# A fused linear attention and gated expert layer: one table of task order and engines replaced by another

## The chip, the cores and the metric

The kernel runs on one core of a Trainium2 chip. The metric is the device time of one execution in microseconds; of several runs the median is given. The core has five engines with queues of their own: TensorE (PE, matmuls), VectorE (DVE), ScalarE (ACT), GpSimd (POOL) and SyncE (SP, which here only issues DMA transfers).

## The reference

Four batches of four heads, 1088 tokens each, head size 32. Keys and queries become 64 features (an outer product of two projections of 8), the keys' features are summed against the values, and a query's features are multiplied by that sum and divided by a denominator. The 4352 tokens x 128 channels that come out are normalized and go through a gated layer with 1536 inner columns.

```python
a = np.einsum('rd,bhsd->bhsr', S1, x)
b = np.einsum('rd,bhsd->bhsr', S2, x)
phi = np.einsum('bhsi,bhsj->bhsij', a, b).reshape(*x.shape[:-1], r * r)
kv = np.einsum('bhsf,bhsd->bhfd', k_p, v)
z = np.sum(k_p, axis=2)
num = np.einsum('bhsf,bhfd->bhsd', q_p, kv)
den = np.einsum('bhsf,bhf->bhs', q_p, z)[..., None] + 1e-06
...
rms = np.sqrt(np.mean(x * x, axis=-1, keepdims=True) + 1e-06)
xn = x / rms * rms_g
g = xn @ w_gate
silu = g * (1.0 / (1.0 + np.exp(-g)))
val = xn @ w_val
return (silu * val @ w_out)
```

## The kernel before

All of the program is one core's. Tokens are worked through in nine chunks (eight of 512 columns, one of 256), the inner columns in twelve groups of 128.

*Attention.* For a batch, the key side loads keys (`kt`) and values (`vt`), projects the keys (L519 for batch 0, L497 for the others), forms features `phi` (L452, L539) and sums them against the values (L531, the "key products"), whose sums are copied to `kv` (L556, L560). For a chunk, the query side projects the queries (L594 for chunks 0 and 1, L622 for the others), forms `phiq` (L452 and transposes L602; or from chunk 2 by a round trip over `far` in HBM, read back as `at` and `bt`, and the product L651), multiplies by `kv` (L678, the "numerators"), adds to the denominator (`den`, L698 or L699), divides, takes the mean square (L709), its root on POOL (L721), scales (`xn`, L724 or L731), and transposes (L758, or over `turned` in HBM) to `x`, which is split into a rounded part `x_hi` and a rest `x_lo`.

*Experts.* A slot is one chunk with one group of inner columns: three matmuls (hi x hi, lo x hi, hi x lo) for the gate `g_ps` and three for the value `v_ps` (L802), silu on ACT (L811, `s`), the product `h` on DVE (L814), a cast to `h_hi` (L350 on ACT or L351 on DVE), a subtraction to `h_lo` (L832 on DVE or POOL) and three output matmuls (L840). The last two groups of the last chunk use a plain f32 `h` (L821). `g_ps` and `v_ps` have two buffers each, so TensorE may run two accumulators of each kind ahead. The weights of a group come as 64-bit words (`w_raw`, L422) and are converted in five steps (`w_top`, `w_full`, `w_hi`, `w_lo`).

*What sets the order.* The program is a list of 1259 tasks. `ORDER` is a permutation of their numbers: instructions are emitted in that order, and each engine runs its own in the order in which they were emitted. `ON` holds one letter (a, d, p for ACT, DVE, POOL) for each task that has more than one possible engine. `Plan.follow` walks through ORDER with a planned occupancy and latency for each task (`Way`); from these planned times come the buffer slot that a tile gets, the waits between DVE and POOL that keep their SBUF instructions apart, and the fillers: where it sees TensorE without work it emits short matmuls on zeros (`keep_warm`, L382). The chip does not read the planned times. Each engine waits for the semaphores of what an instruction needs, and everything queued behind it waits as well.

Of the kernel before, what the change touches and what calls it, by code (L numbers as in the profile page):

```python
# [23 lines left out]
F = R * R  # L24
NT = B * S
P = 128
# [62 lines left out]
"""  # L89
ON = (  # L90
    "dapapadaddaadaadddaaaaapapdapapaadaadaadaapaadaadaadaadaddaadppddaapaadaaddadadadadadadadpdddaadddaaapapadadapapaadapa"
    "pddapapadapadapdpddddpadaaddadaapadaddpddadddadapadapddddadpadaadapaddpadapadddapapddadaaadpdaadpadadapddadddddapdpddd"
    "ddddddaaaapapapddapapdpdpddadaddpadadddaaaddddpapddadaddpadddapaddaddddaaddddpddapadadapadaddddpadpadddadadadadddapdda"
# [204 lines left out]
def attention_then_glu(ctx, tc, kT, v, qT, sw, w, out):  # L298
# [27 lines left out]
    def on_pool(n, emit, against=0):  # L326
        occ = n * 2.17 + 140
        return Way(occ, occ + 45, emit, True, against)
# [58 lines left out]
    def to_f32(n, dst, raw, top, reads, tt, writes):  # L387
# [18 lines left out]
        plan.add({"act": on_act(n, top_act, True), "dve": on_dve(n, top_dve, fast=True, against=100)}, reads, tt)  # L406
# [36 lines left out]
    def product(out, ab, m, writes, away=False):  # L443
# [7 lines left out]
        def outer(eng, a):  # L451
# [8 lines left out]
            "pool": on_pool(m * H * F * 0.85, lambda: outer(nc.gpsimd, both()[:, :m * H]), PHI_POOL),  # L460
        }, [both] if away else [ab, both], writes)

    def kside(b):
# [26 lines left out]
        if b in TURNED:  # L490
# [12 lines left out]
            for p in range(2):  # L503
                def turn(p=p):
                    nc.vector.transpose(out=kab()[:, :, p * NB // 2:(p + 1) * NB // 2], in_=pair[p]()[:, :g])

                dve(g, turn, [pair[p]], [(kab, p)])
        for i, (lo, hi) in enumerate(groups):
# [27 lines left out]
            if b in TURNED:  # L536
                def outer(eng, lo=lo, hi=hi, m=m):
# [9 lines left out]
                    "pool": on_pool(m * H * F * 0.85, lambda outer=outer: outer(nc.gpsimd), PHI_POOL),  # L547
# [24 lines left out]
    def qside(c):  # L572
# [94 lines left out]
        for u in range(0, nt, 2):  # L667
# [36 lines left out]
            for t in range(2):  # L704
                sq = sb("sq", [P, DM], 2)

                def mean(t=t, u=u, sq=sq):
                    one = x()[:, u + t]
                    nc.vector.tensor_tensor_reduce(  # L709
                        out=sq().rearrange("p (h d) -> p h d", h=H), in0=one, in1=one, scale=1.0 / DM, scalar=EPS, op0=ALU.mult, op1=ALU.add,  # L710
                        accum_out=ms()[:, u + t:u + t + 1],
                    )

                plan.add({"dve": Way(265, 345, mean, True)}, [(x, u)], [sq, (ms, u + t)])

        for u, wd in ((0, 2), (2, 2)) if first else ((0, nt),):
# [16 lines left out]
            plan.add({"pool": Way(400 + 150 * wd, 430 + 150 * wd, root)}, [(ms, i) for i in range(u, u + wd)], [(rstd, u)])  # L733
# [37 lines left out]
            plan.add({"act": Way(wd * 107 + 155, wd * 107 + 255, high)}, [*got, "gain"], [(x_hi, u)])  # L771
# [177 lines left out]
```

## Time and profile before

| | us |
|---|---|
| median of 3 runs | 252.35 |
| lowest, highest | 251.72, 253.43 |
| profiled execution | 254.73 |
| its span, first to last instruction | 252.6 |
| TensorE busy in it | 247.5 |
| DVE busy in it | 180.8 |
| ACT busy in it | 132.8 |
| POOL busy in it | 82.1 |

The span lacks the 2.1 us around it that the execution's time includes. An engine's busy time is the union of its instructions. PE is the matmul, PEld its weight load, which overlaps. The granted clock is the share of TensorE's full speed in a stretch.

### The profile page before, as it was taken

What the parts mean: (1) busy time and instruction counts of PE and PEld (TensorE: products, weight loads), DVE (VectorE), ACT (ScalarE), POOL (GpSimd) and SP (SyncE); (2) the same over time, 40 slices, a digit from 0 to 9 for tenths busy, and PEclk for the clock granted to TensorE, in tenths of its full rate; (3) what the DMA queues carried; (4) which work ended last, traced back from release to release, by engine and by line L of the source; (5) the groups of instructions that cost most, each with busy time, mean ns of one, the idle gap of its engine ahead of it and who ended that gap; (6) DMA issues with size and microseconds to landing.
All of it is one profiled execution on the core that took longest, in us unless ns stands there. A gap on an engine that the chain in (4) does not pass through costs nothing.

```text
span 252.6 us, 5870 instructions
## 1 busy us (share of the span) xinstructions
PE 247.5 (98%) x2244; PEld 199.9 (79%) x2244; DVE 180.8 (72%) x410; ACT 132.8 (53%) x287; POOL 82.1 (32%) x80
## 2 busy tenths in 40 slices
PE   7999999999999999999999999999999999999995
PEld 4878788786888788888888788887888888888895
DVE  1589998798566987775677688755679476774772
ACT  3477899744644537641546552644346555345351
POOL 4444332226543423105252401464341212142211
PEclk9799999999999999999999999999999999999999
DMA  6879994371354143330530235142002101020010
GB/s 226 288 245 294 335 273 141 95 212 33 78 170 113 33 123 104 92 96 21 142 89 1 47 93 169 31 127 94 3 0 44 42 3 42 0 84 3 0 42 21
DMA packets 19260, 25.55 MB, mean 101 GB/s; under 512 B 3105, under 2 KB 10657, under 8 KB 19233
## 3 DMA queue, kind: packets, MB, share of 16 engines
q1 hardware_dynamic: 18800, 24.54, 33.5%
q10 hardware_dynamic: 432, 0.66, 0.7%
q8 instruction: 17, 0.28, 0.5%
q14 instruction: 11, 0.08, 0.1%
HBM read 20.40 MB, written 4.78 MB: 100 GB/s over the span
## 4 chain that ended last, share of the span: by engine, by line
PE 96%; DMA 2%; SPq 0%; issue 0%; DVE 0%
PE v_ps L802 29%; PE g_ps L802 28%; PE o_ps L840 28%; PE att L678 3%; DMA q<-qT 2%; PE att L531 2%; PE att L622 1%; PE o_ps L531 1%; PE att L758 1%; PE att L594 1%; PE att L497 1%; PE g_ps L678 0%; PE att L602 0%; PE g_ps L602 0%; PE v_ps L678 0%; PE att L821 0%
## 5 line engine op out<-in xcount | busy, mean ns | idle before, releaser
L814 DVE TENSOR_TENSOR h<-v_ps,s 128x512 f32<-128x512 f32 (+2 forms) x110 | 69.8, 647 | 39.8 <-PE v_ps L802 27.5
L811 ACT ACTIVATE s<-g_ps 128x512 f32<-128x512 f32 (+1 forms) x108 | 61.0, 574 | 70.4 <-PE g_ps L802 37.7
L832 POOL TENSOR_TENSOR h_lo<-h,h_hi 128x512 fp32r<-128x512 f32 (+1 forms) x42 | 53.0, 1270 | 104.4 <-DVE h_lo L832 43.8
L350 ACT CAST h_hi<-h 128x512 fp32r<-128x512 f32 (+1 forms) x70 | 41.4, 602 | 19.9 <-DVE h L814 17.5
L832 DVE TENSOR_TENSOR h_lo<-h,h_hi 128x512 fp32r<-128x512 f32 (+1 forms) x64 | 41.4, 652 | 5.5 <-ACT h_hi L350 3.6
L802 PE MATMUL v_ps<-x_hi,w_hi 128*128 128x512 f32 (+1 forms) x110 | 41.9, 381 | 0.0
L802 PE MATMUL g_ps<-x_hi,w_hi 128*128 128x512 f32 (+1 forms) x110 | 41.8, 381 | 0.0
L802 PE MATMUL v_ps<-x_hi,w_lo 128*128 128x512 f32 (+1 forms) x110 | 41.6, 379 | 0.0
L802 PE MATMUL g_ps<-x_hi,w_lo 128*128 128x512 f32 (+1 forms) x110 | 41.6, 378 | 0.0
L802 PE MATMUL g_ps<-x_lo,w_hi 128*128 128x512 f32 (+1 forms) x110 | 41.5, 378 | 0.0
L802 PE MATMUL v_ps<-x_lo,w_hi 128*128 128x512 f32 (+1 forms) x110 | 41.3, 378 | 0.0
L840 PE MATMUL o_ps<-h_hi,w_hi 128*128 128x512 f32 (+1 forms) x106 | 40.9, 386 | 0.0
L840 PE MATMUL o_ps<-h_hi,w_lo 128*128 128x512 f32 (+1 forms) x106 | 40.8, 385 | 0.0
L840 PE MATMUL o_ps<-h_lo,w_hi 128*128 128x512 f32 (+1 forms) x106 | 40.8, 385 | 0.0
L802 PEld LDWEIGHTS v_ps<-x_hi,w_hi 128*128 128x128 f32 x110 | 20.7, 188 | 5.0 <-DVE w_lo L436 0.5
L802 PEld LDWEIGHTS g_ps<-x_hi,w_hi 128*128 128x128 f32 x110 | 20.7, 188 | 4.6
L802 PEld LDWEIGHTS v_ps<-x_hi,w_lo 128*128 128x128 f32 x110 | 20.7, 188 | 4.3
L802 PEld LDWEIGHTS g_ps<-x_hi,w_lo 128*128 128x128 f32 x110 | 20.7, 188 | 4.2
L802 PEld LDWEIGHTS g_ps<-x_lo,w_hi 128*128 128x128 f32 x110 | 20.6, 188 | 4.2
L802 PEld LDWEIGHTS v_ps<-x_lo,w_hi 128*128 128x128 f32 x110 | 20.5, 188 | 4.1
L840 PEld LDWEIGHTS o_ps<-h_lo,w_hi 128*128 128x128 f32 x106 | 19.9, 188 | 4.4
L840 PEld LDWEIGHTS o_ps<-h_hi,w_hi 128*128 128x128 f32 x106 | 19.9, 188 | 4.2
(112 smaller groups left out, 249.5 us busy)
## 6 DMA issues: line engine op xcount, KB each, us to landing
w_raw<-w SPq DMA_DIRECT2D x12, 384.0 KB
bt<-far SPq DMA_DIRECT2D x24, 128.0 KB
at<-far SPq DMA_DIRECT2D x12, 256.0 KB
q<-qT SPq DMA_DIRECT2D x7, 256.0 KB
turned<-xq SPq DMA_DIRECT2D x24, 64.0 KB
xt<-turned SPq DMA_DIRECT2D x6, 256.0 KB
outT<-o_sb SPq DMA_DIRECT2D x10, 128.0 KB
vt<-v SPq DMA_DIRECT2D x4, 272.0 KB
```

The costliest lines, as they stand in the source:

```text
L350: "act": on_act(n, lambda: nc.scalar.copy(out=out(), in_=in_()), True),
L497: nc.tensor.matmul(out=pair[p]()[a * D:(a + 1) * D, :g], lhsT=sblk[p * HALF:(p + 1) * HALF, p * NB // 2:(p + 1) * NB // 2], rhs=kt()[p * H ...
L531: nc.tensor.matmul(out=kvv[r0:r0 + wide, h // 2, :], lhsT=phi()[:, t, h * F + f:h * F + f + wide], rhs=vt()[:, t, h, :], start=(t == 0 and ...
L594: nc.tensor.matmul(out=ab()[hf * HALF:(hf + 1) * HALF, t * HALF:(t + 1) * HALF], lhsT=q()[:, s1:s1 + HALF], rhs=sblk, start=True, stop=True,)
L622: nc.tensor.matmul(out=accs[p]()[a * D:(a + 1) * D, :m], lhsT=sab[rows, p].rearrange("p c o r -> p (c o r)"), rhs=q()[rows, a * m:(a + 1) ...
L678: nc.tensor.matmul(out=nv[n0:n0 + wide, t, p, :], lhsT=phi()[:, p, l0:l0 + wide], rhs=kvs[(s0 + l0) // S][:, p, :], start=True, stop=True,)
L758: nc.tensor.transpose(out=xt()[:, t * P:(t + 1) * P], in_=xn()[:, t * DM:(t + 1) * DM], identity=ident)
L802: nc.tensor.matmul(out=acc()[:, cs], lhsT=wt[:, j, i3, :], rhs=x()[:, cs], start=(i == 0), stop=(i == 2))
L811: act(n, lambda: nc.scalar.activation(out=s()[:, :n], in_=gps()[:, :n], func=AF.Silu), cols(gps, whole[0]), [s])
L814: cs.stop - cs.start, lambda cs=cs: nc.vector.tensor_tensor(out=h()[:, cs], in0=vps()[:, cs], in1=s()[:, cs], op=ALU.mult),
L832: eng.tensor_tensor(out=h_lo()[:, :n], in0=h()[:, :n], in1=h_hi().bitcast(F32)[:, :n], op=ALU.subtract)
L840: nc.tensor.matmul(out=o_ps()[:, :n], lhsT=wt[:, j, 2, :], rhs=x()[:, :n], start=first and i == 0, stop=last and i == 2,)
```

## The change

Planned durations are altered in eight places (the conversion of weights on ACT, two products on POOL, the transposes on DVE, the mean square, the root on POOL, and the two parts of `x`), and the tables ORDER and ON are replaced. The code that the tasks emit is the same.

```diff
 ORDER = """
-1 0 2 6 9 3 14 10 15 4 32 33 7 37 16 5 64 34 18 38 19 12 26 27 22 20 146 39 28 147 11 23 24 151 35 40 41 65 17 13 148 21 25 36 29 152 153 149 66 72 67 30 73
...
+0 1 2 6 3 14 9 15 18 4 19 16 10 32 33 34 37 38 20 7 26 39 64 11 22 27 23 28 151 146 72 8 35 36 40 17 12 21 24 25 73 152 74 13 29 147 148 65 66 41 243 75 30 31
...
 ON = (
-    "dapapadaddaadaadddaaaaapapdapapaadaadaadaapaadaadaadaadaddaadppddaapaadaaddadadadadadadadpdddaadddaaapapadadapapaadapa"
...
+    "dapdpdddpadadaadadaaadapadaapddaadaadaadaapaadaapdadaadadpaaddppddadaddaaddadadadadadadaddpadaaddadaadddapapadddaaddda"
...
-        plan.add({"act": on_act(n, top_act, True), "dve": on_dve(n, top_dve, fast=True, against=100)}, reads, tt)
+        plan.add({"act": on_act(1.36 * n, top_act, True), "dve": on_dve(n, top_dve, fast=True, against=100)}, reads, tt)
...
-            "pool": on_pool(m * H * F * 0.85, lambda: outer(nc.gpsimd, both()[:, :m * H]), PHI_POOL),
+            "pool": on_pool(m * H * F * 0.8, lambda: outer(nc.gpsimd, both()[:, :m * H]), PHI_POOL),
...
-                dve(g, turn, [pair[p]], [(kab, p)])
+                dve(g + 14, turn, [pair[p]], [(kab, p)])
...
-                plan.add({"dve": Way(265, 345, mean, True)}, [(x, u)], [sq, (ms, u + t)])
+                plan.add({"dve": Way(215, 297, mean, True)}, [(x, u)], [sq, (ms, u + t)])
...
-            plan.add({"pool": Way(400 + 150 * wd, 430 + 150 * wd, root)}, [(ms, i) for i in range(u, u + wd)], [(rstd, u)])
+            plan.add({"pool": Way(150 + 270 * wd, 180 + 270 * wd, root)}, [(ms, i) for i in range(u, u + wd)], [(rstd, u)])
...
-            plan.add({"act": Way(wd * 107 + 155, wd * 107 + 255, high)}, [*got, "gain"], [(x_hi, u)])
-            dve(wd * P * 1.12, lambda low=low: low(nc.vector), [*got, "gain", (x_hi, u)], [(x_lo, u)], spread)
+            plan.add({"act": Way(wd * 118 + 140, wd * 118 + 240, high)}, [*got, "gain"], [(x_hi, u)])
+            dve(wd * P * 1.2, lambda low=low: low(nc.vector), [*got, "gain", (x_hi, u)], [(x_lo, u)], spread)
```

The three places below show what the tables move. Names carry a running number of the tile.

TensorE at the start, from the first filler on (g_ps and v_ps of L519: projections of batch 0's keys; att of L594: projections of the query chunks 0 and 1, `q_109` in two halves). Before:

```order
L382 MATMUL o_ps_97<-const-float32-0.0 1x96
L519 MATMUL g_ps_124<-sblk,kt_106 64x64 x2
L382 MATMUL o_ps_97<-const-float32-0.0 1x32
L594 MATMUL att_130<-sblk,q_109 64x64 x4
L382 MATMUL o_ps_97<-const-float32-0.0 1x128
L594 MATMUL att_144<-sblk,q_109 64x64 x4
L519 MATMUL v_ps_151<-sblk,kt_106 64x64 x6
L519 MATMUL v_ps_162<-sblk,kt_106 64x64 x4
L519 MATMUL g_ps_170<-sblk,kt_106 64x64 x6
```

And now:

```order
L382 MATMUL o_ps_97<-const-float32-0.0 1x96
L519 MATMUL g_ps_124<-sblk,kt_106 64x64 x2
L519 MATMUL v_ps_129<-sblk,kt_106 64x64 x6
L594 MATMUL att_141<-sblk,q_109 64x64 x4
L594 MATMUL att_148<-sblk,q_109 64x64 x4
L519 MATMUL v_ps_156<-sblk,kt_106 64x64 x4
L519 MATMUL g_ps_167<-sblk,kt_106 64x64 x6
```

The second key projection of six matmuls moved ahead of both query halves, and two fillers are gone (a third, ahead of the first expert matmuls, is gone too).

TensorE in the expert stage, at the key projection of batch 3 (L497). Before, it stands alone between expert matmuls:

```order
L802 MATMUL g_ps_1029<-x_lo_530,w_hi 128x512
L497 MATMUL att_1037<-kt_740,sblk 32x288 x4
L497 MATMUL att_1042<-kt_740,sblk 32x288 x4
L802 MATMUL v_ps_1052<-x_hi_521,w_hi 128x512
L802 MATMUL v_ps_1052<-x_hi_521,w_lo 128x512
```

And now:

```order
L802 MATMUL g_ps_1088<-x_lo_426,w_hi 128x512
L497 MATMUL att_1096<-kt_953,sblk 32x288 x4
L497 MATMUL att_1101<-kt_953,sblk 32x288 x4
L531 MATMUL att_1111<-vt_379,phi_826 32x34 x48
L678 MATMUL att_1170<-kv_75,phiq_1034 32x66 x16
L531 MATMUL att_1111<-vt_379,phi_826 32x34 x24
L678 MATMUL att_1217<-kv_75,phiq_1034 32x66 x16
L802 MATMUL g_ps_1237<-x_hi_515,w_hi 128x512
```

It moved to the front of a block of key products (L531) and numerators (L678), which had stood elsewhere with a query projection.

POOL, from the last weight group on (h_lo: the subtraction of L832; phiq and phi: products of queries and keys; rstd: the root). Before:

```order
L436 TENSOR_TENSOR w_lo<-w_full_580,w_hi 128x384
L832 TENSOR_TENSOR h_lo_750<-h_718,h_hi_728 128x512
L832 TENSOR_TENSOR h_lo_802<-h_723,h_hi_738 128x512
L832 TENSOR_TENSOR h_lo_939<-h_815,h_hi_930 128x512
L832 TENSOR_TENSOR h_lo_969<-h_854,h_hi_885 128x512
L721 TENSOR_TENSOR rstd_1035<-ms_998,mhalf 128x4
L832 TENSOR_TENSOR h_lo_1050<-h_843,h_hi_949 128x512
L539 TENSOR_TENSOR phi_989<-kab_552 128x768
```

And now:

```order
L832 TENSOR_TENSOR h_lo_891<-h_799,h_hi_875 128x512
L436 TENSOR_TENSOR w_lo<-w_full_865,w_hi 128x384
L651 TENSOR_TENSOR phiq_1034<-at_923,bt_887 128x512
L721 TENSOR_TENSOR rstd_1049<-ms_980,mhalf 128x4
L539 TENSOR_TENSOR phi_826<-kab_576 128x768
L539 TENSOR_TENSOR phi_1187<-kab_1138 128x768
L832 TENSOR_TENSOR h_lo_1241<-h_1106,h_hi_1136 128x512
```

POOL now has a query product ahead of the root, and two key products behind it; it has fewer subtractions there.

## Rows read from the trace of the kernel before

**Rows 1.** The page, part 1: engine, busy us (share of span), instructions.

```profile
PE 247.5 (98%) x2244; PEld 199.9 (79%) x2244; DVE 180.8 (72%) x410; ACT 132.8 (53%) x287; POOL 82.1 (32%) x80
```

**Rows 2.** The page, part 2: granted clock in 40 slices, 9 is 90% or more.

```profile
PEclk9799999999999999999999999999999999999999
```

**Rows 3.** Windows: us, busy (instructions) of PE, PEld, DVE, ACT, POOL, clock, DMA.

```profile
6.74:9.36 2.62, 2.62 (x57) 2.50 (x57) 1.38 (x2) 1.17 (x5) 1.32 (x1) 0.64 1.02 383
9.36:13.30 3.94, 3.94 (x82) 3.74 (x80) 2.73 (x4) 1.45 (x4) 1.26 (x2) 0.81 0.78 228
...
18.85:47.35 28.50, 28.50 (x301) 22.84 (x302) 26.25 (x54) 23.46 (x50) 8.73 (x9) 1.00 0.74 232
47.35:90.00 42.65, 42.65 (x540) 33.46 (x539) 32.39 (x78) 23.38 (x50) 18.35 (x14) 1.00 0.44 115
90.00:240.00 150.00, 150.00 (x1036) 121.41 (x1035) 105.31 (x226) 71.74 (x145) 44.99 (x36) 1.00 0.22 59
240.00:252.60 12.60, 9.85 (x81) 9.52 (x79) 6.39 (x20) 4.67 (x13) 1.45 (x2) 1.00 0.10 31
```

**Rows 4.** Waits of TensorE: who, for whom: us in total, times, longest.

```profile
PE att L594 <- DMA q<-qT: 1.4, 1, 1.4
```

**Rows 5.** Timeline of TensorE, start: start us, us, instruction, count.

```profile
7.02 0.91 PE L519 MATMUL v_ps<-sblk,kt 128*64 128x64 f32 x20
...
8.35 1.07 PE L594 MATMUL att<-sblk,q 128*64 128x64 f32 x16
...
9.36 1.12 PE L602 MATMUL g_ps<-ident,at 128*128 128x128 f32 x4
```

**Rows 6.** Timeline of DVE, start; in brackets idle before, and what ended it.

```profile
7.54 0.69 DVE L452 TENSOR_TENSOR at<-att,both 128x512 f32<-128x512 f32 x1 [1.47 <-ACT both L344]
...
13.42 0.22 DVE L556 COPY kv<-o_ps 64x66 f32<-64x66 f32 x1 [0.45 <-PE att L531]
...
14.64 0.17 DVE L698 TENSOR_SCALAR den<-g_ps 128x8 f32<-128x8 f32 x1
```

**Rows 7.** Timeline of TensorE around three blocks of small matmuls.

```profile
47.53 0.39 PE L802 MATMUL g_ps<-x_lo,w_hi 128*128 128x512 f32 x1
...
49.24 0.40 PE L840 MATMUL o_ps<-h_hi,w_lo 128*128 128x512 f32 x1
...
57.18 0.39 PE L802 MATMUL g_ps<-x_lo,w_hi 128*128 128x512 f32 x1
...
58.49 0.41 PE L802 MATMUL v_ps<-x_hi,w_lo 128*128 128x512 f32 x1
...
85.41 0.39 PE L840 MATMUL o_ps<-h_lo,w_hi 128*128 128x512 f32 x1
...
87.54 0.39 PE L802 MATMUL g_ps<-x_hi,w_lo 128*128 128x512 f32 x1
```

**Rows 8.** Groups by shape: count | busy us, mean ns of one | idle before.

```profile
L651 DVE TENSOR_TENSOR phiq<-at,bt 128x512 f32<-128x512 f32 x10 | 6.8, 684 | 0.1
L539 POOL TENSOR_TENSOR phi<-kab 128x768 f32<-128x768 f32 x4 | 6.0, 1520 | 3.0 <-DVE xq L740 1.7 <-DVE w_lo L436 1.3
L539 DVE TENSOR_TENSOR phi<-kab 128x768 f32<-128x768 f32 x5 | 4.7, 946 | 0.2 <-POOL h_lo L832 0.2
L651 POOL TENSOR_TENSOR phiq<-at,bt 128x512 f32<-128x512 f32 x2 | 2.6, 1294 | 8.9 <-DVE h_lo L832 5.9 <-DVE ms L709 3.0
```

**Rows 9.** Timeline of DVE and TensorE at the end.

```profile
247.55 0.89 DVE L814 TENSOR_TENSOR h<-v_ps,s 128x128 f32<-128x128 f32 x4 [0.95 <-PE v_ps L802]
...
248.79 1.05 PE L821 MATMUL att<-h,w_f 128*128 128x128 f32 x8
```

**Rows 10.** Timeline of SP's DMA issues, two in succession.

```profile
35.66 0.92 SPq L628 DMA_DIRECT2D far<-abt  x2
46.77 0.56 SPq L640 DMA_DIRECT2D at<-far  x1
```

**Rows 11.** Waits of DVE: who, for whom: us in total, times, longest.

```profile
DVE h L814 <- POOL h_lo L832: 3.0, 3, 1.2
```

More of the change, by code (lines that the diff above doesn't have):

```diff
@@ L54 @@
 ORDER = """
[34 rows of a table removed]
[34 rows of a table added]
 """
 ON = (
-    "dapapadaddaadaadddaaaaapapdapapaadaadaadaapaadaadaadaadaddaadppddaapaadaaddadadadadadadadpdddaadddaaapapadadapapaadapa"
-    "pddapapadapadapdpddddpadaaddadaapadaddpddadddadapadapddddadpadaadapaddpadapadddapapddadaaadpdaadpadadapddadddddapdpddd"
-    "ddddddaaaapapapddapapdpdpddadaddpadadddaaaddddpapddadaddpadddapaddaddddaaddddpddapadadapadaddddpadpadddadadadadddapdda"
+    "dapdpdddpadadaadadaaadapadaapddaadaadaadaapaadaapdadaadadpaaddppddadaddaaddadadadadadadaddpadaaddadaadddapapadddaaddda"
+    "papadadadadapaddpadpppadaadpdaaapaddpapadddapdpadapadddaaappdddddaddddpdpadapdpaddpapadadddpadaddapadddadaddpadaddddpa"
+    "pddappdaaddadddddapddadddadddapadaaapdadaapapapapapddapapaddddpddaaapddadpddddddddadadadadapapadadpdpaddpddapdpadapapa"
 )
@@ L546, in kside @@
                     "dve": on_dve(m * H * F, lambda outer=outer: outer(nc.vector), True),
-                    "pool": on_pool(m * H * F * 0.85, lambda outer=outer: outer(nc.gpsimd), PHI_POOL),
+                    "pool": on_pool(m * H * F * 0.8, lambda outer=outer: outer(nc.gpsimd), PHI_POOL),
                 }, [(kab, 0), (kab, 1)], [(phi, i)])
```

66 rows, old and new, of the table ORDER are left out of this document.

## The prediction

> **What bounds the kernel now.** I read the page first. TensorE is busy 98% of the span, VectorE (DVE) 72%, ScalarE (ACT) 53%, GpSimd (POOL) 32% [rows 1]; the reader is to see that only TensorE can set the time, and that a new order can win only what TensorE does not spend on matmuls. The slices say where that is: the granted clock falls below full in one slice near the start and is full everywhere else [rows 2]. So next the windows [rows 3]: from 18.85 to 240 us TensorE is busy without a hole (28.50 of 28.50 us in the row shown, and the same in the stretches behind it), so the expert stage, nine tenths of the kernel, holds no wait worth searching for. Idle time is left in the start (1.40 us in one wait of TensorE for the second half of the first query chunk [rows 4]) and in the drain after the last matmul (12.60 − 9.85 = 2.75 us).
>
> The start also loses clock. Between 6.74 and 13.30 us TensorE is busy all the time, but at a mean granted clock of 0.64 and then 0.81 [rows 3], that is partly at 1.2 GHz instead of 2.4 GHz. That costs (1 − 0.64) × 2.62 + (1 − 0.81) × 3.94 = 0.94 + 0.75 = 1.7 us. It comes right behind the wait that ended at 6.74.
>
> The profiled execution took 254.73 us, 2.4 us above the median of the runs (252.35). Without its wait and its slow clock it would have taken 254.73 − 1.4 − 1.7 = 251.6, close to the lowest run (251.72). So I read the spread of the runs (251.72 to 253.43) as this start, with the query half sometimes late and sometimes not; that is an estimate, since one trace shows one start. My terms are made against 254.73 and then carried over to the median.
>
> **The change part by part.** The edited constants (1.36, 0.8, 14, 215, 270, 118 and so on) set only planned times; no instruction reads them. What reaches the chip is ORDER and ON: which engine does a task, and in which order. The counts of real matmuls are equal, so everything is about waits and about switches between kinds of matmuls.
>
> *Start.* Before, TensorE fills its wait for the second query half with a filler and then does six key matmuls behind it; now these six stand ahead of both query products, and no filler is left. Behind the wait, the sixteen key matmuls that stand there now run from 7.02 to 8.35 us [rows 5], 83 ns each; the first ten of them, from 7.02, go faster. Six are 0.4 to 0.5 us. I take 0.4 as won, because TensorE is the bound from 6.74 to 13.30: the transposes at 9.36 [rows 5] follow the products at 8.35 directly, and the product they need was finished by DVE at 7.54 + 0.69 = 8.23 [rows 6]. If in other runs the query half comes in time and the clock is full, that DVE product becomes the bound and the win goes to 0; so the bounds are 0 and 0.5. Behind the key products the chain goes on to the first denominators at 14.64 [rows 6]. Between the copy of the key sums at 13.42 and these, DVE now has one weight conversion and a product of 0.69, where it had a cast, a conversion and some idle time; it fits into the 1.22 us. SP now issues a 384 KB weight load ahead of the last two values loads instead of one. Those values are used in the second half of the key products, so I cost this at nothing; were that cover gone, it would cost one such transfer, 393 KB at 383 GB/s [rows 3], 1.0 us.
>
> *Switches.* A block of small matmuls inside the expert stage costs more than its matmuls. With 0.23 us from one expert matmul's start to the next [rows 7], the lone key block takes 58.49 − 0.23 − (57.18 + 0.23) = 0.85 us; the lone numerator block 49.24 − 0.23 − (47.53 + 0.23) = 1.25; a query block joined to a numerator block 87.54 − 0.23 − (85.41 + 0.23) = 1.67, so joining costs 0.42 where standing alone costs 0.85. The changed order joins the lone key block to key products and numerators and has eight such blocks where there were nine. It wins up to 0.43; a query block now stands behind a key product instead of ahead of it, which no row prices, so the bounds are 0 and 0.45 and I take 0.3.
>
> *Work between engines.* Of the query products of 512 columns, POOL now does seven (two before) and DVE five (ten); of the key products of batches 1 to 3, POOL six (four) and DVE three (five). Per piece POOL takes 1.294 and 1.520 us, DVE 0.684 and 0.946 [rows 8]. POOL gains 5 × 1.294 + 2 × 1.520 = 9.5 us of work, DVE loses 5 × 0.684 + 2 × 0.946 = 5.3. Casts, copies and subtractions change hands by ones and twos (POOL gives five subtractions of 512 columns back for five of 256). I cost all this at 0: POOL has 170 us idle, and the products are due where TensorE has tens of expert matmuls in front of it. What would be late next if the cover failed is h, for which TensorE holds two accumulators of each kind. The only stretch with little cover is 18.85 to 47.35, with DVE busy 26.25 of 28.50 us [rows 3]; no query product is moved to POOL there.
>
> The Trainium skill (Perfetto Trace Analysis, Optimizing Scalar/DVE Operations) warns that GpSimd and VectorE share an SBUF read port, so that moving work between these two might not help. By that rule the 5.3 us would not be relief; the sum stays the same, as DVE is not the bound, and the rule's own outcome is a rival below.
>
> *SP.* Half of the wide operand of chunk 2 now stands behind a values load that waits for a buffer. The operand is used by the numerators behind the expert matmul of 47.53 [rows 7], and before, SP had issued all of it long ahead and then nothing from 36.6 to 46.8 us [rows 10]; the delay fits in there, so 0.
>
> *End.* Nine output matmuls of 256 columns now follow the last expert pair, where twelve did. The last DVE products ran 247.55 to 248.44 and TensorE came to them at 248.79 [rows 9], 0.35 us to spare, which three matmuls fewer (3 × 0.12) use up. I take 0 and keep 0.2 as the bound.
>
> **Sum:** −0.4 − 0.3 = −0.7 us: 254.0 for an execution like the profiled one, and 252.35 − 0.7 = **251.7 us** for the median.
>
> **Rivals.**
> 1. *Nothing reaches the end.* The start is set by loads and by the DVE product instead of TensorE's issue, and the switches cost the same in the other order. For: the wait of 1.40 is a transfer's, which the order does not shorten. Against: TensorE is solid from 6.74 to 13.30. Time: 252.4.
> 2. *A slower start.* With the fillers gone, TensorE stands idle longer before the query half, and more runs get the slow clock behind it. For: the profiled clock drop of 1.7 us follows a 1.40 us wait. Against: the six key matmuls take the fillers' place. Time: 252.35 + 1.7 − 0.7 = 253.4. The Trainium skill (TensorE: Matmul & The Clock Gate, Part 1) states that the low clock is the default and that activity releases it; by that rule removed fillers can only hurt, and the trace agrees as far as its drop stands behind idleness.
> 3. *POOL holds DVE* (slower by over 1%). A DVE instruction on SBUF operands stands still until a POOL product ends; the seven moved products hold it for 9.5 us in all. In the trace DVE did wait for POOL's h_lo, 3.0 us in three waits ahead of h alone [rows 11], and none of it reached TensorE. It decides from the point where DVE has no slack behind a product, with h and then the v accumulator late; with one third reaching TensorE that is 3.2 us: 252.35 + 3.2 − 0.7 = 254.9.
> 4. *The start is healed.* Most runs lose neither the wait nor the clock. Time: 251.72 − 0.7 = 251.0, or 251.72 − 0.95 = 250.8 with the upper bounds of both gains. For over 1% (below 249.8) another 1.0 us would have to come out of a start in which little else is idle.
>
> **How the numbers follow.** Chances: forecast 0.55, rival 1 0.20, rival 2 0.11, rival 3 0.07, rival 4 0.07. A change of 1% is 2.5 us, about what a measurement of this kernel can tell from no change. Rivals 1 and 2 stay inside it, rival 3 goes over it, rival 4 hardly reaches it: faster 0.03, same 0.89, slower 0.08. Range: downward rival 4 with the upper bounds (250.8), and 0.4 less, since three runs need not have shown the best start: 250.4; upward rival 2 with its bounds at zero gain (252.35 + 1.7 = 254.0, rounded down to 253.8). Outside lie most of rival 3 and the far end of rival 4.
>
> **What would show it.** Right: the expert stage without a hole from its first matmul to about 247 us; key matmuls of the first batch in front of the query products; the first expert matmul 0.4 us earlier if query half and clock come as before, some 3 us earlier if neither is lost; eight blocks of small matmuls, the one with key products and numerators joined. Rival 2: a clock row below 0.9 for longer than now in the first 15 us. Rival 3: waits of TensorE for DVE's h in the expert stage. The forecast is wrong if TensorE shows waits of more than 0.5 us in all in that stretch, or if the last DVE products end after the output matmuls by more than 0.2 us.

## The result and the profile after

The change is slower: 254.38 us (median of 22 runs, 252.46 to 256.97) against 252.42 (22 runs, 251.72 to 253.92); ratio 1.0076, 95% interval 1.006 to 1.0093. The forecast of 251.7 us had the wrong sign, and the result lies above its range. Ratios, here and below, leave out disturbed executions, such as two of the six in the last experiment (258.07 and 1361.36 us).

| | before | change |
|---|---|---|
| median, us | 252.42 | 254.38 |
| profiled execution, time and span, us | 254.73, 252.6 | 252.46, 250.6 |
| two more looks at the change, time and span | | 253.99, 252.2 and 254.31, 252.5 |
| one more look at the kernel before | 252.46, 250.3 | |

The two profiled executions mislead as a pair: that of before is above all of its 22 runs, that of the change is the fastest of its 22. So the reading below leans on further looks (a look is one more profiled execution), taken as the first experiments. Here is the change's first profile: engines, granted clock, then windows that answer to [rows 1 to 3].

```profile
PE 246.1 (98%) x2238; PEld 198.4 (79%) x2238; DVE 178.4 (71%) x409; ACT 130.6 (52%) x277; POOL 88.1 (35%) x88
...
PEclk9999999999999999999999999999999999999999
```

```profile
6.74:9.36 2.62, 2.62 (x66) 2.38 (x62) 2.41 (x7) 1.73 (x4) 1.39 (x2) 1.00 1.02 380
9.36:13.30 3.94, 3.62 (x89) 2.89 (x87) 3.52 (x13) 2.13 (x7) 0.73 (x1) 1.00 1.02 366
...
18.85:47.35 28.50, 28.22 (x364) 21.63 (x363) 26.75 (x52) 20.93 (x44) 8.36 (x8) 1.00 0.70 207
47.35:90.00 42.65, 42.53 (x467) 33.60 (x466) 30.49 (x73) 22.88 (x48) 20.90 (x17) 1.00 0.40 98
90.00:240.00 150.00, 150.00 (x1042) 121.94 (x1041) 103.92 (x225) 71.65 (x143) 46.37 (x40) 1.00 0.21 58
```

The start has lost its slow clock (1.00 where [rows 3] had 0.64 and 0.81), VectorE gave work to GpSimd (180.8 to 178.4 us and 82.1 to 88.1), and the expert stage has two small holes, 0.28 and 0.12 us. Four of TensorE's five waits in the same execution (the fifth is 0.2 as well):

```profile
PE o_ps L382 <- PEq L942: 0.8, 1, 0.8
PE g_ps L802 <- DVE w_lo L436: 0.3, 1, 0.3
PE att L594 <- DMA q<-qT: 0.2, 1, 0.2
PE g_ps L678 <- DVE kv L556: 0.2, 1, 0.2
```

Nothing in it is slow. The one new wait of the expert stage is for w_lo, at 30 us, behind a weights load; that gave the first theory.

The words used below: a **border** is a place in TensorE's instruction stream where one transfer of instructions ends and the next begins. The page of every run lists these transfers as queue q8, kind "instruction": 17 packets, 0.28 MB, so 16 KB each (18 packets in the two runs with 64 matmuls added). In the block of small matmuls at 60 us one matmul follows the other after 9 to 45 ns on average, among expert matmuls after 230.

### The profile page after: what moved, and what is told of

Its sections match the earlier page's. It is cut to its first block, busy times and chain, and to the rows that moved or that the text cites. A ratio compares the mean times of both kernels' runs of the same rounds, so it can differ in the third digit from the quotient of the medians.

```text
span 250.6 us, 5848 instructions
## 1 busy us (share of the span) xinstructions
PE 246.1 (98%) x2238; PEld 198.4 (79%) x2238; DVE 178.4 (71%) x409; ACT 130.6 (52%) x277; POOL 88.1 (35%) x88
## 4 chain that ended last, share of the span: by engine, by line
PE 87%; DMA 9%; DVE 2%; ACT 1%; SPq 1%; issue 0%
PE o_ps L840 28%; PE g_ps L802 27%; PE v_ps L802 27%; DMA w_raw<-w 7%; PE att L678 3%; DMA kt<-kT 1%; PE att L531 1%; PE att L622 1%; SPq L482 0%; DVE w_full L396 0%; PE att L821 0%; DVE h L814 0%; DVE at L452 0%; PE att L497 0%; PE att L602 0%
## 5 line engine op out<-in xcount | busy, mean ns | idle before, releaser
L832 POOL TENSOR_TENSOR h_lo<-h,h_hi 128x512 fp32r<-128x512 f32 (+1 forms) x42 | 50.2, 1201 | 86.9 <-DVE h_lo L832 31.8
L350 ACT CAST h_hi<-h 128x512 fp32r<-128x512 f32 (+1 forms) x67 | 39.7, 602 | 26.4 <-DVE h L814 23.4
L832 DVE TENSOR_TENSOR h_lo<-h,h_hi 128x512 fp32r<-128x512 f32 (+1 forms) x64 | 42.2, 673 | 8.6 <-POOL h_lo L832 4.2
L802 PE MATMUL v_ps<-x_hi,w_hi 128*128 128x512 f32 (+1 forms) x110 | 42.1, 382 | 0.0
L802 PE MATMUL g_ps<-x_hi,w_lo 128*128 128x512 f32 (+1 forms) x110 | 41.7, 380 | 0.3 <-DVE w_lo L436 0.3
L802 PE MATMUL g_ps<-x_hi,w_hi 128*128 128x512 f32 (+1 forms) x110 | 41.7, 380 | 0.0
L802 PE MATMUL v_ps<-x_hi,w_lo 128*128 128x512 f32 (+1 forms) x110 | 41.6, 378 | 0.0
L802 PE MATMUL v_ps<-x_lo,w_hi 128*128 128x512 f32 (+1 forms) x110 | 41.4, 377 | 0.0
L802 PE MATMUL g_ps<-x_lo,w_hi 128*128 128x512 f32 (+1 forms) x110 | 41.3, 377 | 0.0
L802 PEld LDWEIGHTS v_ps<-x_hi,w_hi 128*128 128x128 f32 x110 | 20.7, 188 | 5.3 <-DVE h L814 0.6
L802 PEld LDWEIGHTS g_ps<-x_hi,w_lo 128*128 128x128 f32 x110 | 20.7, 188 | 4.7 <-DVE w_lo L436 0.8
L802 PEld LDWEIGHTS g_ps<-x_hi,w_hi 128*128 128x128 f32 x110 | 20.7, 188 | 4.6 <-ACT w_hi L350 0.2
L802 PEld LDWEIGHTS v_ps<-x_hi,w_lo 128*128 128x128 f32 x110 | 20.7, 188 | 4.0
L802 PEld LDWEIGHTS v_ps<-x_lo,w_hi 128*128 128x128 f32 x110 | 20.7, 188 | 3.9
L802 PEld LDWEIGHTS g_ps<-x_lo,w_hi 128*128 128x128 f32 x110 | 20.6, 188 | 3.9
## 6 DMA issues: line engine op xcount, KB each, us to landing
at<-far SPq DMA_DIRECT2D x12, 256.0 KB
q<-qT SPq DMA_DIRECT2D x7, 256.0 KB
xt<-turned SPq DMA_DIRECT2D x6, 256.0 KB
```

Source lines behind the costliest of these rows:

```text
L350: "act": on_act(n, lambda: nc.scalar.copy(out=out(), in_=in_()), True),
L802: nc.tensor.matmul(out=acc()[:, cs], lhsT=wt[:, j, i3, :], rhs=x()[:, cs], start=(i == 0), stop=(i == 2))
L832: eng.tensor_tensor(out=h_lo()[:, :n], in0=h()[:, :n], in1=h_hi().bitcast(F32)[:, :n], op=ALU.subtract)
```

## The experiments

Line numbers move by one between these kernels (an expert product is L801, L802 or L803). Times in the trace are from the span's start. Theory A: a weights load lands late and TensorE waits for its conversion. B: VectorE and GpSimd hold each other, and TensorE waits for h or a product. C: the start is slower.

### The change twice more, and the kernel before once more

> The changed kernel once more, unchanged, to see a run nearer to its median of 254.4 us than the profiled 252.46. Theory A (a weights load lands late): one to three TensorE waits, 1.5 to 3 us together, between 26 and 34 us, behind w_lo or w_full whose DMA w_raw landed 0.5 to 2 us later than in the profiled run; nothing over 0.3 us later. Theory B (more on POOL and DVE): waits of 0.3 to 1 us spread over 47 to 240 us that end by DVE or POOL. Theory C (start): the first 128x512 expert matmul 1.5 to 2.5 us later than 16.4 us, by a slower clock or a late q or at.

> The same kernel a second time, since a delay that comes by chance shows in some runs alone. Theory A: TensorE's waits at the same place (26 to 34 us), of another size than in the first look, and the time follows the size. Theory B: the same waits over 47 to 240 us in both. Theory C: the first expert matmul late in both.

Measured 253.99 and 254.31 us. TensorE's waits in the second look, all that the view gives:

```profile
PE att L678 <- issue: 1.8, 1, 1.8
PE o_ps L382 <- PEq L942: 0.8, 1, 0.8
PE att L594 <- DMA q<-qT: 0.4, 1, 0.4
PE att L531 <- issue: 0.2, 1, 0.2
```

(In the first look the L678 wait is 1.5.) "issue" means that no semaphore, engine or transfer in the trace explains the wait. TensorE's timeline around it, and the count of its matmuls in windows up to the stop and beyond it:

```profile
59.11 0.40 PE L802 MATMUL g_ps<-x_lo,w_hi 128*128 128x512 f32 x1
59.43 0.72 PE L497 MATMUL att<-kt,sblk 64*32 64x288 f32 x16
60.08 1.00 PE L531 MATMUL att<-vt,phi 128*32 128x34 f32 x94
...
60.92 0.51 PE L678 MATMUL att<-kv,phiq 128*32 128x66 f32 x19
63.22 0.37 PE L678 MATMUL att<-kv,phiq 128*32 128x66 f32 x10 [1.79 <-issue]
```

```profile
0.00:59.11 59.11, 57.58 (x722) 44.87 (x722) 51.24 (x129) 38.32 (x89) 20.48 (x31) 1.00 0.73 230
59.11:61.21 2.10, 2.10 (x133) 1.31 (x132) 2.10 (x5) 0.90 (x2) 1.46 (x1) 1.00 0.39 75
61.21:63.22 2.01, 0.22 (x15) 0.06 (x3) 0.41 (x1) 0.83 (x2) 2.01 (x3) 1.00 0.33 62
```

TensorE stops in the middle of one numerator product, at about its 854th matmul, some 130 into a block of 224 small ones (16 for keys, 144 for key products, 64 for numerators). Both looks stop at the same matmul: from one start to the next it is 1.69 and 2.01 us instead of 0.01. Neither shows a wait at 30 us: **A falls** as the cause, and B and C with it, since no wait for VectorE or GpSimd passes 0.2 us and the experts start at 16.58. What does happen there is on q8. The DMA view of 60.5 to 62.0 us, second look (slices of 0.04 us; then queue: packets, MB, share of 16 engines):

```profile
q1 hardware_dynamic: 254, 0.11, 39.0%
q8 instruction: 1, 0.02, 5.8%
```

Single packets in the trace give its time: 60.57 to 61.96 us, and TensorE goes on 1.26 us after its end. In the first look it is 60.43 to 61.49, and 1.33 us; in the change's fastest execution 59.48 to 60.43, and the stop there is 0.3 us long. **Theory D**: TensorE uses up its instructions in the dense block before the next 16 KB are in.

> The kernel before once more, since its one profiled run (254.73 us) was 2.3 us above its median. If its start of 19.05 us to the first expert matmul (a q wait of 1.4 us and 3.4 us of the 1.2 GHz clock) was that run's own misfortune, this run starts the experts at 16.5 to 17.5 us and takes 252.0 to 252.8 us: then the change had nothing to gain in the start. If 19 us are the rule, the change gains over 2 us there and loses some 4 later.

Measured 252.46 us. Its waits, and the first expert matmul:

```profile
PE o_ps L382 <- PEq L942: 0.8, 1, 0.8
PE att L594 <- DMA q<-qT: 0.5, 1, 0.5
PE g_ps L519 <- DVE sblk L396: 0.2, 1, 0.2
```

```profile
16.61 0.39 PE L802 MATMUL v_ps<-x_hi,w_hi 128*128 128x256 f32 x1
```

The change has that matmul at 16.40, 16.58 and (second look) 16.51 us: the start of 19.05 us in the profile of before, an execution slower than all of the 22 runs, did not come back, and there was next to nothing to gain.

### Moving the border: more matmuls ahead of the block

Tiny matmuls of 8 columns, into an accumulator that is free, are put in at 36 us, between two expert groups. They change nothing but the count (12 calls are 24 matmuls):

```diff
         end, out = self.follow(clock0, filler)
+        out = sorted(out + [(36000, 12)], key=lambda x: x[0])
...
-        for cols in [P] * k if name else [k * P // 4]:
+        for cols in [8] * k if name else [k * P // 4]:
```

> The two looks at the change stalled TensorE once, for 1.5 and 1.8 us without a shown releaser, at 61 us inside the joined block of 224 small matmuls, at the 853rd matmul; the block starts with the 722nd, and the 16 KB instruction transfer for TensorE (queue q8) ended only at 61.5 and 62.0 us. New theory D (instruction supply): matmul instructions come in transfers of 128 matmuls, and the block eats one faster than the next arrives; where the borders lie in the block decides. Here 12 tiny fp32 matmuls (24 matmul records, 8 columns, into an unused accumulator) are added at about 36 us in the expert stage, so the block starts 24 matmuls later in the count and the border falls earlier in it. D: no wait at 61 us, 252.3 to 252.9 us in spite of 0.3 to 0.5 us for the added matmuls. Theories A (late weights), B (VectorE/GpSimd): 254.4 to 254.9 us.

> The change with 6 tiny fp32 matmuls (12 records) at 36 us: the block of 224 then starts with the 734th matmul, where the kernel before starts its own block of 224, instead of the 722nd. Theory D: the transfer for the border is asked for 12 expert matmuls (2.7 us) earlier against the block, more than the 1.3 to 2.0 us that the stalled runs lacked: no stall at 61 us in the profile, 252.3 to 252.9 us. Without D: 254.4 to 254.7 us.

> The same with 32 tiny matmuls (64 records). D: the border that stalled lies 64 matmuls deep in the block and its transfer is in long before; the next border lies 192 deep, and is asked for inside the block: the stall moves to the end of the block (second numerator product or the last key/value product), 0.8 to 2.5 us; time 253.5 to 256. A and B: the same waits as in the looks before, 254.8 to 255.5, with the stall (if any) still at the first numerator product.

> The kernel before with 32 tiny matmuls (64 records) at 36 us, as in the run of the change with 64. Theory D: the kernel before is spared by where its borders fall and by nothing else, so it now stalls too: the border at the 978th matmul comes 180 deep in its block of 224 at 61 to 64 us and is asked for inside it; a wait with no shown releaser of 0.8 to 2.2 us at matmul 978 to 982, and another at 114 to 118 us; 254.5 to 258 us. If the change's block is at fault by its make-up (key block with it), the kernel before takes its padding without a stall: 253.0 to 253.6 us.

| matmuls added | to | us | ratio to before, 95% |
|---|---|---|---|
| 12 | the change | 252.68 | 0.9994 (0.9968 to 1.0019) |
| 24 | the change | 252.76 | 1.0019 (0.999 to 1.0049) |
| 64 | the change | 258.37 (one run) | |
| 64 | the kernel before | 258.16 (one run) | |

Padding itself costs 0.47, 0.77 and 1.77 us in the timeline (start of the matmul ahead of it to start of the one behind, less 0.23). So 12 added matmuls take the change's loss away, and 64 bring 4 us. (The expectation for 12 puts the block of before at the 734th matmul; by count it begins with the 732nd, so 12 go three beyond it.) Waits with 12, with 64 in the change, with 64 in the kernel before:

```profile
PE o_ps L383 <- PEq L943: 0.8, 1, 0.8
PE att L595 <- DMA q<-qT: 0.4, 1, 0.4
```

```profile
PE att L532 <- issue: 2.2, 1, 2.2
PE att L679 <- issue: 2.0, 1, 2.0
```

```profile
PE att L679 <- issue: 1.9, 1, 1.9
PE att L532 <- issue: 1.8, 1, 1.8
```

And the count up to the first of these stops, change and before with 64:

```profile
0.00:61.27 61.27, 59.58 (x786) 46.82 (x786) 51.84 (x129) 38.49 (x89) 20.41 (x31) 1.00 0.71 222
61.27:63.73 2.46, 2.46 (x197) 1.99 (x197) 2.29 (x6) 1.35 (x3) 2.22 (x2) 1.00 0.57 113
63.73:65.92 2.19, 0.22 (x18) 0.05 (x6) 0.00 (x0) 1.01 (x3) 2.19 (x3) 1.00 0.02 4
```

```profile
0.00:60.00 60.00, 58.99 (x786) 45.88 (x787) 47.96 (x117) 41.30 (x97) 22.45 (x33) 1.00 0.70 222
60.00:64.49 4.49, 4.49 (x198) 3.57 (x197) 3.86 (x9) 2.14 (x6) 1.51 (x1) 1.00 0.32 64
64.49:66.60 2.11, 0.22 (x13) 0.06 (x2) 0.86 (x2) 0.41 (x1) 1.62 (x2) 1.00 0.51 140
```

Two windows that touch both count the matmul on their common edge. Each counted once, the stops come after matmul 982 in the change and 983 in the kernel before, and after 854 in the looks: 128 and 129 further. That is one transfer, if 16 KB hold 128 matmuls with their weight loads. The instruction packets end at 64.58 and 65.27 us, 1.34 and 1.36 us before TensorE goes on. The sums nearly close: 256.6 − 250.3 = 6.3 us of span against 1.77 + 2.19 + 2.39 = 6.35 (the second stop, at 118 us), and 256.0 − 250.3 = 5.7 against 1.77 + 2.14 + 1.98 = 5.89. D is shown: neither the order of work nor the load moved here, only where the borders lie, and the kernel before is as exposed as the change. The expectation for 64 in the change was too low at 253.5 to 256: it counted one stop. That for the kernel before (254.5 to 258) counted two and was passed by 0.2.

All fourteen traces together show what orders the stops at 60 and at 115 us: how deep the border lies in its block of small matmuls (224 of them, 208 in one case), counted from the block's first matmul to the one after which stops come (854, 982, 1364, 1493, within two). At 107 to 124 deep (before's order, 12 or 24 added, the next experiment at 60 us) none of eleven crossings stops. At 131 to 134 (the change's order) twelve of thirteen do, for 0.2 to 2.0 us; at 187 to 198 (64 added) all four, for 2.0 to 2.4. Depth is not all: at 28 us, in a block of 160, a border some 110 deep stopped TensorE for 0.6 us in one trace (of the stores moved later), and its packet had started late there too.

### Taking the key block out again

```diff
 PE tasks around 55 to 60 us:
-... 375 346 338 339 330 337 359 416 236 ...
+... 375 346 416 338 339 330 337 359 236 ...
```

> The change with one TensorE item moved back: the key block of 16 matmuls (L497, at 59.4 us) goes five expert groups earlier, as the kernel before had it apart, so that the small matmuls at 60 us are a block of 208 instead of 224. It costs one more block of small matmuls (0.33 us in the rows before and after). Theory D: the border at the 850th matmul then lies 112 into the block and its transfer has 0.7 us more, a little over what the stalled runs lacked 1.3 to 2.0 us of: the stall shrinks by 0.5 to 2 us, 252.6 to 254.0 us. If the prediction's own step was right (joining gives 0.3 us), 254.7 us.

In this kernel and in those of the next experiment and of the earlier weights the planner's constant GAP is raised as well, so that it adds no fillers; their traces count 2238 matmuls, as the change's do. Measured 252.77 us, ratio 1.0005 (0.9984 to 1.0027). The only stop left is at the border of 114 us, 0.4 us by the view. At 60 us the instruction packet is in early: the DMA view of 55.0 to 57.2 us holds nothing else, and it lies at slice 21 of 40, 56.1 us.

```profile
PE o_ps L381 <- PEq L941: 0.8, 1, 0.8
PE att L530 <- issue: 0.4, 1, 0.4
PE att L593 <- DMA q<-qT: 0.2, 1, 0.2
```

```profile
DMA  0000000000000000000090000000000000000000
GB/s 0 0 0 0 0 0 0 0 0 0 0 0 0 0 0 0 0 0 0 0 298 0 0 0 0 0 0 0 0 0 0 0 0 0 0 0 0 0 0 0
...
q8 instruction: 1, 0.02, 2.7%
```

The stop went wholly, more than expected, since the packet came over 4 us sooner and not 0.7. So the order is a second handle beside the count. How it acts is not shown: here, and in the traces with before's order, a key block of its own stands 4 to 6 us ahead of the dense block, and the transfer comes early in all four; but in this trace it starts (56.14 us) before that key block does (56.43).

### Is it the traffic beside it?

One VectorE instruction moves, so that SP's four stores to turned come later:

```diff
 DVE tasks from 57 us:
-... 235 273 373 341 417 418 348 ...
+... 235 373 341 417 418 273 348 ...
```

> The change with one VectorE instruction moved: the transpose into xq of chunk 2 (58.6 us) goes behind the two key transposes, some 2 us later, and with it SP's four stores of 64 KB in 512-byte packets, whose packets stood on the DMA engines from 59.9 us, just ahead of the late instruction transfer (60.43 and 60.57 us; 59.48 us in the run without the stall). D with contention: the instruction transfer starts by 59.5 in each run, the stall is 0.4 us or less, 252.4 to 253.2 us. D without contention (the transfer is asked for late, by chance): the stall stays, 254 to 255 us.

Measured 253.85 us, ratio 1.0051 (1.0034 to 1.0069). The stop stays at 1.5 us, though the stores are now issued at 62.12, behind it. The DMA view of 61 to 62 us:

```profile
PE att L677 <- issue: 1.5, 1, 1.5
```

```profile
DMA  9000000000000000000000000000000000000000
GB/s 655 0 0 0 0 0 0 0 0 0 0 0 0 0 0 0 0 0 0 0 0 0 0 0 0 0 0 0 0 0 0 0 0 0 0 0 0 0 0 0
DMA packets 1, 0.02 MB, mean 16 GB/s; under 512 B 0, under 2 KB 0, under 8 KB 0
```

The instruction packet starts at 61.01 with no other packet on the DMA engines from 2.5 us before it to its end, so contention with these stores is not what makes it late. (The time is 0.15 us under the 254 to 255 expected for that outcome.)

### Theory A's own tests: SP's order

Three weights loads go four, seven and nine places earlier in SP's order (the expectation misstates the first and the last of these); and, apart from that, in the kernel before SP's first 49 issues are put in the order that the change gives them. It is not the change's start in full: one values load and two query loads that the change has among its own first 49 stay behind.

```diff
 SP tasks, the change:
-... 131 79 84 229 228 249 230 89 248 134 250 133 433 99 247 551 94 104 ...
+... 131 79 84 89 229 228 99 94 249 230 248 134 250 133 433 247 551 104 ...
 SP tasks, the kernel before (the first places that differ):
-... 64 12 11 65 13 72 243 ...
+... 64 11 72 12 13 65 243 ...
```

> The changed kernel with one thing moved: on SP three weights loads (the fifth, sixth and seventh) are issued one, seven and five places earlier, ahead of q, values and far stores; order on TensorE, DVE, ACT and POOL as in the change. Theory A: 251.5 to 252.8 us, TensorE without a wait over 0.5 us from 26 to 34 us. Theories B and C: 254.2 to 254.6 us, as the change.

> The kernel with the three weights loads issued earlier once more, since its median (253.06) lies between before and the change: its first profile had a stall of 0.2 us at 61 us, its instruction transfer having started at 59.39. If the earlier weights bring the transfer forward, again 59.5 or before, a stall under 0.5 us, 252.4 to 253.3 us. If that was chance, 60.4 to 60.6, a stall of 1.5 to 2 us, and about 254 us.

> The kernel before with SP's first 49 issues in the order that the change gives them, all other engines as before. Theory A: slower than before by 0.8 to 2.5 us (253.2 to 255), with TensorE waits behind w_raw loads between 26 and 36 us. Theories B and C: 252.2 to 252.6, as before.

Earlier weights: 253.06 us, ratio 1.003 (1.0007 to 1.0053), and one more look of 253.43. The median lies between A's 251.5 to 252.8 and the 254.2 and more of the others, and the traces do not bear A out: the instruction packet starts at 59.39 and 59.26 us and the stop at 61 us is 0.2 and 0.3 us, so what these two looks won is D's. (The second took 0.1 more than its expectation's upper end; it waits 0.6 us for values in the start, and 0.5 at the border of 115 us.) Why loads issued before 31 us would move a transfer at 59 us is not shown, and it may be chance: in the change's own fastest execution the packet started at 59.48.

The kernel before with the change's SP order: ratio 1.0043 (1.0028 to 1.0058), the four runs in it 253.2 to 254.9 us. That is the time that A expected, but not in the place that A expected: of the 2.6 us by which the span grew, 1.7 are lost in the start, where the experts now begin at 18.32 instead of 16.61 us. From 26 to 36 us no wait stands in the view; matmul for matmul 0.6 us goes there in gaps of at most 0.2.

```profile
PE att L593 <- DMA q<-qT: 1.0, 2, 0.8
PE o_ps L381 <- PEq L941: 0.8, 1, 0.8
PE g_ps L677 <- DVE kv L555: 0.6, 1, 0.6
```

So that order is not free where the rest of the start is not arranged for it. In the change itself it costs nothing that the start shows.

## Why the prediction was wrong

**The step that failed** is *Switches*, with the sentence on which it stands, that the expert stage "holds no wait worth searching for". It priced the joined block by its matmuls and switches alone: up to 0.43 us won, 0.3 taken. The block before held as many matmuls (a query block stood where the key block now stands), but it began with the 732nd matmul at 60.84 us in the further look; now it begins with the 723rd, at 59.35 to 59.71. Of the nine fewer ahead of it six are the fillers taken out of the start, and three are one expert group. And no key block of its own stands ahead of it any more, as it does in all four traces without added matmuls in which the transfer for this border came early, 1.0 to 2.0 us after the matmul 148 ahead of it. The border, 131 matmuls deep in the block where it had been 122 deep, then fell where the instructions had not come. Price: 1.68 and 2.00 us in the two looks, and 0.54 and 0.40 more at the border of 115 us, 2.2 and 2.4 in all. The median lost 1.96. The prediction had no term for instructions at all, though the page lists the 17 packets of q8, and the planner's code counts them (AHEAD 62, FETCHED 210, BLOCK 128, ASK, FETCH). By these constants a border comes every 128 matmuls, at the 850th here, a packet is asked for 148 matmuls ahead of it, and it takes 2600 + 2400 ns to arrive. That the 148th matmul is the one that asks is the planner's assumption, which no run tests; no packet of these traces starts before it. With the border put at the 851st matmul (the stop itself shows after the 854th), the time from the 148th ahead of it to the packet's end is 7.0 and 7.3 us in the stopped looks, 5.5 in the fastest execution of the change, and 3.1 and 2.6 in the kernel before.

The Trainium skill (Runtime: NRT & Kernel Launch, Instruction fetch mechanics) states that an engine's instructions are refilled in 16 KiB blocks of 256 while it runs, and that crossing a border is mostly hidden. The traces agree with the size (16 KB each) and with "mostly" (17 stops in the 14 traces, of over 200 crossings); in the blocks of small matmuls the crossing cost up to 2.4 us.

**The bound and the expert stage.** That TensorE alone sets the time was right. That nothing is idle between 18.85 and 240 us was right of the one execution shown [rows 3], but a full stretch in one order says nothing of another order: the time from a packet's end to the matmul that needs it (3.7 and 4.2 us at this border in the two traces of before, below 0 in the stopped ones) is not a row of any view.

**Start, −0.4.** Not there: 16.61 us before, 16.40 to 16.58 after. The price came from a start with a wait of 1.4 us and a slow clock, which the further look has not. The prediction named this case, a DVE product as the bound and no gain, and still took 0.4.

**Work between engines, 0; SP, 0; end, 0.** No wait of TensorE for DVE or POOL passed 0.3 us in three traces of the change: 0 was right, and rival 3 wrong. For SP, 0 held in the change. The whole rest of the change is small: 252.2 − 250.3 − 2.2 = −0.3 us in the first look, 252.5 − 250.3 − 2.4 = −0.2 in the second, against the −0.7 forecast. Whether the 0.3 for fewer switches is in it no run separates.

**Rivals.** None is the mechanism found. Rival 1 (252.4) is where the change ends without its stops: 252.68 with 0.47 us of padding in it. Rival 2 did not come: the clock rows are full in the change's starts. The test named in the prediction, waits of over 0.5 us in the expert stage, tells right from wrong here, but only in the looks: the first profile has 0.4.

No version beats the kernel before: the two mended ones are equal to it within 0.3%.

## What to carry to other kernels

Before dense blocks of small matmuls are moved or joined, count TensorE's matmuls up to them: in this kernel a border of the instruction stream 107 to 124 matmuls deep in the dense blocks at 60 and 115 us cost nothing, one 131 to 198 deep up to 2.4 us, and a dozen matmuls more or less ahead of the block decide. In the trace look for a wait on "issue" and for the q8 packet that ends just before it. And take more than one profile: two executions at opposite ends of their spreads hid a loss of 0.8%.

## What had not been expected of the hardware

- An instruction packet takes 0.9 to 1.9 us for its 16 KB, and TensorE goes on 1.1 to 1.6 us after its end (17 stops in these traces).
- How late the packet starts varies, also where no other packet is near: 0.8 us at the least, 5.9 at the most, after the 148th matmul ahead of its border (the border counted as above). At the 60 us border it was 4.2 to 5.9 in six traces with the change's order on TensorE, 4.7 and 5.0 with 12 and 24 matmuls added, and 1.0 to 2.0 in the three of before's and in the one with the key block apart. What sets this is open; traffic of the turned stores is excluded.
- Twelve matmuls of 8 columns, 0.47 us of extra work, made the changed kernel 1.7 us faster.
